# Two tiles of x transposed on the PE, four PSUM banks for the first dense layer, and gate_w on SyncE's queue

## The chip, the core and the metric

The kernel runs on one core of a Trainium2 chip. The metric is the device time of one execution in microseconds. Before the change it is 751.95 us, the median of three runs (751.55 to 753.9).

## What is computed

`x` is [2048, 512] in bf16; the reference is condensed here. The result is a mix of two branches, weighted per row by a gate:

```python
g = _sigmoid((x * gate_w).sum(-1, keepdims=True))
a = _A_ref(x, A_mem0, A_Wq, A_Wk, A_Wv, A_Wo, A_seg_len)   # 64 segments of 32 rows, one after the other
b = _B_ref(x, B_w1, B_b1, B_w2, B_b2)                      # layernorm, 512 -> 1376, gelu, 1376 -> 512
return g * a + (1 - g) * b

# inside _A_ref, for each segment s: 8 memory rows ahead of 32 rows of x
h = jnp.concatenate([mem, xs], axis=1)
q, k, v = h @ Wq, h @ Wk, h @ Wv                           # 32 heads of 128
p = _softmax(where(mask, q @ k.T * scale, -1e9))
o = (p @ v) @ Wo
mem = o[:, :M, :]                                          # feeds the next segment
outs.append(o[:, M:, :])

# inside _B_ref
y = _layernorm(x, axis=-1)
h = _gelu(jnp.einsum('bsd,df->bsf', y, w1) + b1)
return jnp.einsum('bsf,fd->bsd', h, w2) + b2
```

## The kernel before

The program has two stages. The **dense stage** computes branch b. The **recurrent stage** runs over the 64 segments in order; it starts with the projections of tile 0 and takes most of the time. Each engine works its own instruction list in the order in which the code is written; an instruction that must wait holds up all that stands behind it on its engine. Transfers are issued from the lists of SyncE (SP), ScalarE (ACT) and GpSimd (POOL), and their data pass through the same 16 DMA engines.

The dense stage takes x in 16 tiles `T` of 128 rows, two tiles to a block, so 8 blocks of 11 units `fc` (128 of the 1376 hidden columns each). A unit is:

- `a_mm(blk, fc)`, L477: four matmuls of 128x256 into a PSUM bank `hp` (L482), then the gelu on ACT (L483), which frees the bank. Blocks 0 to 6 take turns between the banks `SbF` and `W` (`U[3]` once in block 0); block 7 uses four banks.
- `b_mm(blk, fc)`, L485, issued two units later (`LAG = 2`): for a tile whose second layer is done here, one matmul of 128x512 (L489) that reads the gelu of `fc` and adds into `U[0]` or `U[2]`. The odd tiles and tile 14 (`DEF`) put their gelu into DRAM instead (`spill`, L499, on SP) and take the second layer in the recurrent stage.

At a block's border ACT has two instructions more: the tanh of the gate (`gates`, L469) and `ct_out` (L504), which takes the block's result out of PSUM. DVE makes the next block's normalised rows (`prep`: L437 statistics, a short chain of small operations, `y` at L452). PE transposes `y` into `X1` and `X2` at `fc` 8 and 9 (`prep_tr`, L459), DVE copies that to `yT` (L460), and then DVE forms the gate sums of the block (`junk`, L465, which reads `gw_bc`, the copy of `gate_w` in all partitions).

SP's list in a block: a spill, two loads of recurrent weights of 1024 KB (`loads`, L321), the second spill, two tiles of x for the block after the next (`ld_x`, L317). In block 3 `loads` also issues two DMA transposes (`load_xT`, L102) that bring tiles 0 and 1 of x in transposed form to `xT[0]` and `xT[1]`. The recurrent stage reads them: `first_h` (L507), issued in block 6, has PE transpose the start memory `m0` into the bank `X1`, DVE copy it to `hT` (L511), and POOL copy parts of `xT`.

At the start of the program PE runs 11 matmuls on the identity (`warm`, L526), which compute nothing that is used, then the transposes of `y` of tiles 0 and 1, one of `b1r` (the bias, L535, loaded by POOL), and one more `warm` ahead of the first `a_mm`. POOL also loads `gw_bc` (L344).

Of the kernel before, what the change touches and what calls it, by code (L numbers as in the profile page):

```python
# [10 lines left out]
BF16 = mybir.dt.bfloat16  # L11
# [17 lines left out]
def kernel(ctx, tc, A_x, A_mem0, A_Wq, A_Wk, A_Wv, A_Wo, A_seg_len, B_x, B_w1, B_b1, B_w2, B_b2, gate_w, out):  # L29
    nc = tc.nc  # L30
    P = 128
    _, S, Dm = A_x.shape
# [6 lines left out]
    KC = Dm // P  # L39
# [23 lines left out]
    ident = pers.tile([P, P], BF16)  # L63
# [11 lines left out]
    ew = early.enter_context(tc.tile_pool(name="ew", bufs=2))  # L75
# [24 lines left out]
    def load_xT(T):  # L100
        xT = ew.tile([P, KC, P], BF16, tag="xT", bufs=3, name="xT")
        nc.sync.dma_start_transpose(out=xT[:], in_=x2[T * P:(T + 1) * P, :])  # L102
        xTs[T] = xT
# [7 lines left out]
    U = [lps.tile([P, 512], FP32, name=f"U{i}") for i in range(4)]  # L111
    X1 = lps.tile([P, 512], FP32)
    X2 = lps.tile([P, 512], FP32)
    SbF = lps.tile([P, 512], FP32)
    W = lps.tile([P, 512], FP32)
# [48 lines left out]
    xTs, GLs = {}, {}  # L164
# [136 lines left out]
    with tc.tile_pool(name="mlpw", bufs=1) as mlpw, \  # L301
# [4 lines left out]
        NBLK = NT // TB  # L306
# [4 lines left out]
        gw_bc = mlpw.tile([P, Dm], BF16)  # L311
        hTm = [mout.tile([P, TB, FC, P], BF16, name=f"hTm{i}") for i in range(2)]
        xts = {}
# [6 lines left out]
        def ld_w(W_, A, n):  # L320
            nc.sync.dma_start(W_[:, n, :], A[n * P:(n + 1) * P].rearrange("p h e -> p (h e)"))  # L321

        def ld_o(i):
            nc.sync.dma_start(Wo_sb[:, i:i + 8, :], A_Wo[i:i + 8].rearrange("h e d -> e h d"))
# [7 lines left out]
        NWARM = 11  # L332
        H1, H2, F1 = 3, 6, 7 * P

        def ld_w2(eng, a, b):
            eng.dma_start(w2_sb[:, a:b, :], B_w2[a * P:b * P, :].rearrange("(fc p) d -> p fc d", p=P))
# [4 lines left out]
        ld_x(3)  # L341
        ld_w2(nc.sync, H1, H2)
        nc.sync.dma_start(w1_sb[:, :, F1:F], w1v[:, :, F1:F])
        nc.gpsimd.dma_start(gw_bc[:], gate_w.partition_broadcast(P))  # L344
        ld_w2(nc.sync, H2, H2 + 2)
        ld_w2(nc.sync, H2 + 2, FC - 1)
        nc.sync.dma_start(w2_sb[:FR, FC - 1, :], B_w2[(FC - 1) * P:F, :])
        nc.sync.dma_start(w2_sb[FR:FR + 1, FC - 1, :], B_b2.rearrange("(o d) -> o d", o=1))
        ld_x(4)
# [7 lines left out]

        def loads(blk):
            if blk == 3:
                for T in range(2):  # L360
                    load_xT(T)
                nc.sync.dma_start(m0[:], A_mem0[0])

            for kc in range(2 * blk, min(2 * blk + 2, 3 * KC)):
                ld_w(*((Wv_sb, A_Wv), (Wq_sb, A_Wq), (Wk_sb, A_Wk))[kc // KC], kc % KC)
            if blk == 6:
                for i in range(0, H, 8):
                    ld_o(i)
# [48 lines left out]
        def rsqrt(y, v, n):  # L417
            i1 = msmall.tile([P, n], I32, tag="i1", name="i1")
            nc.vector.tensor_scalar(out=i1[:], in0=v.bitcast(I32), scalar1=1, scalar2=None, op0=ALU.logical_shift_right)
            nc.vector.tensor_scalar(out=y.bitcast(I32), in0=i1[:], scalar1=-1, scalar2=RSQRT_SEED, op0=ALU.mult, op1=ALU.add)  # L420
            for c, a in ((-1.0, RSQRT_A), (-RSQRT_B * RSQRT_B, 5.0)):
                t = msmall.tile([P, n], FP32, tag="nt", name="nt")
                nc.vector.tensor_tensor(out=t[:], in0=y, in1=y, op=ALU.mult)
                nc.vector.scalar_tensor_tensor(out=t[:], in0=t[:], scalar=c, in1=v, op0=ALU.mult, op1=ALU.mult)
                if a == 5.0:
                    nc.vector.scalar_tensor_tensor(out=t[:], in0=t[:], scalar=10.0 / 3.0, in1=t[:], op0=ALU.add, op1=ALU.mult)
                nc.vector.scalar_tensor_tensor(out=y, in0=t[:], scalar=a, in1=y, op0=ALU.add, op1=ALU.mult)
# [3 lines left out]
        def prep(blk):  # L431
            mv = msmall.tile([P, TB, nc.vector.BN_AGGR_DIM], FP32, tag="mv", name="mv")
            ve = msmall.tile([P, TB], FP32, tag="ve", name="ve")
            rs = msmall.tile([P, TB], FP32, tag="rs", name="rs")
            for tt in range(TB):
                st = msmall.tile([P, nc.vector.BN_STATS_DIM], FP32, tag="st", name="st")
                nc.vector.bn_stats(out=st[:], in_=xts[blk * TB + tt][:])  # L437
                nc.vector.bn_aggr(out=mv[:, tt, :], in_=st[:])
                if blk == 0:
                    nc.vector.tensor_scalar(out=ve[:, tt:tt + 1], in0=mv[:, tt, 1:2], scalar1=LN_EPS, scalar2=None, op0=ALU.add)  # L440
                    nc.scalar.activation(out=rs[:, tt:tt + 1], in_=ve[:, tt:tt + 1], func=ACTF.Sqrt)
            if blk == 0:
                nc.scalar.activation(out=dummy[:], in_=ident[:, 0:1], func=ACTF.Gelu_apprx_tanh)
            else:
                nc.vector.tensor_scalar(out=ve[:], in0=mv[:, :, 1], scalar1=LN_EPS, scalar2=1.0 / (RSQRT_K * RSQRT_K), op0=ALU.add, op1=ALU.mult)
                rsqrt(rs[:], ve[:], TB)
            for tt in range(TB):
                T = blk * TB + tt
                if blk == 0:
                    nc.vector.reciprocal(out=rs[:, tt:tt + 1], in_=rs[:, tt:tt + 1])  # L450
                ys[T] = mwork.tile([P, Dm], BF16, tag="y", name="y")
                nc.vector.tensor_scalar(out=ys[T][:], in0=xts[T][:], scalar1=mv[:, tt, 0:1], scalar2=rs[:, tt:tt + 1], op0=ALU.subtract, op1=ALU.mult)  # L452
            yTs[blk] = mwork.tile([P, KC, TB * P], BF16, tag="yT", name="yT")
# [23 lines left out]
        def a_mm(blk, fc):  # L477
            rows = min(P, F - fc * P)
            n = blk * FC + fc
            hp = (SbF, W, U[3], SbF)[n] if n < 4 else (W, SbF, U[2], U[3])[n % 4] if blk == NBLK - 1 else (W, SbF)[n % 2]  # L480
            for kc in range(KC):
                nc.tensor.matmul(hp[:rows, 0:TB * P], lhsT=w1_sb[:, kc, fc * P:fc * P + rows], rhs=yTs[blk][:, kc, :], start=(kc == 0), stop=(kc == KC - 1))  # L482
            nc.scalar.activation(out=hTm[blk % 2][:rows, :, fc, :], in_=hp[:rows, 0:TB * P].rearrange("p (t c) -> p t c", t=TB), func=ACTF.Gelu_apprx_tanh, bias=b1_sb[:rows, fc:fc + 1], scale=1.0)  # L483
# [40 lines left out]
        def warm(n):  # L524
            for _ in range(n):
                nc.tensor.matmul(U[3][:].rearrange("p (a b) -> p a b", a=4), lhsT=ident[:], rhs=ident[:].unsqueeze(1).to_broadcast([P, 4, P]), start=True, stop=True, skip_group_check=True)  # L526

        warm(NWARM)
        prep(0)
        for tt in range(TB):  # L530
            prep_tr(0, tt)
# [221 lines left out]
    for s in range(nseg):  # L753
        T, si = divmod(s, SPT)
# [188 lines left out]
    with tc.If(n_bad > 0, label="general"):  # L943
        with tc.tile_pool(name="gp", bufs=1) as gp, tc.tile_pool(name="gps", bufs=2, space=PSUM) as gps:
# [29 lines left out]
            with tc.For_i(0, NT) as Ti:  # L974
                nc.sync.dma_start(x_sb[:], x2[bass.ds(Ti * P, P), :])
                xo = gps.tile([P, Dm], FP32, tag="xo", bufs=1, name="xo")
                for si in range(SPT):
                    xp = gps.tile([P, KC, seg], BF16, tag="m", name="xpg")
# [81 lines left out]
```

## Time and profile before

| | us |
|---|---|
| median of 3 runs (lowest, highest) | 751.95 (751.55, 753.9) |
| the profiled execution, whole | 755.67 |
| its span, first to last instruction | 753.8 |
| dense stage within the span, to the first projection of tile 0 (L147 at 69.39) | 69.4 |
| ACT busy, DVE busy, POOL busy over the span | 535.6, 399.5, 274.2 |
| DMA | 77.17 MB, mean 102 GB/s |

The profile times one execution; the 1.9 us between its span and its whole time lie around the span. Of the rows that the prediction quotes, the timeline's have the start, the duration, the engine, the line, the operation and the tiles (buffer numbers left out); `x4` means four instructions merged into one row, and brackets at the end say how long the engine had been idle and what ended that. A matmul's duration holds the time until its result has drained, so a row of PE may end after the next one started: the pace of PE is read from starts. PEld is the weight load of PE. In the windows view each row has a stretch, the busy time of PE, PEld, DVE, ACT and POOL with their counts, then the granted TensorE clock, the DMA engines' mean share, and GB/s.

### The profile page before, as it was taken

To read this page: it belongs to the slowest core of one execution; us is meant where nothing else is said; L and a number is where in the kernel's file an instruction comes from. 1 tells how busy PE (TensorE), PEld (TensorE's weight loads), DVE (VectorE), ACT (ScalarE), POOL (GpSimd) and SP (SyncE) were. 2 spreads that over 40 slices of the span, in tenths; PEclk is the share of its full clock that TensorE was granted. 3 is DMA by queue.
4 is the path that set the end of the run, shared out by engine and by line. 5 is a ranking of instruction groups with operands and counts; after the bars stand their busy time and mean duration, and the time that the engine had idled before them with its cause. 6 is when DMAs were issued, how large, how long until landed. Compare 5 with 4: busy or idle time off the path is not lost.

```text
span 753.8 us, 45384 instructions
## 1 busy us (share of the span) xinstructions
PE 736.0 (98%) x19896; PEld 429.8 (57%) x19896; DVE 399.5 (53%) x1415; ACT 535.6 (71%) x1627; POOL 274.2 (36%) x516
## 2 busy tenths in 40 slices
PE   8999999999999999999999999999999999999996
PEld 5776555555555555555555565555555655555553
DVE  6776555446454554445554545445464545555444
ACT  5777667777776776777777777767777777777663
POOL 4001323444324444334433344333443334433341
PEclk9999999999999999999999999999999999999999
DMA  9999323122321323221322313231323222222321
GB/s 312 343 335 362 104 85 87 55 76 72 93 77 46 91 70 96 69 83 53 92 77 80 86 46 93 68 96 67 70 72 86 79 72 78 57 90 74 95 70 37
DMA packets 69997, 77.17 MB, mean 102 GB/s; under 512 B 34873, under 2 KB 59938, under 8 KB 68258
## 3 DMA queue, kind: packets, MB, share of 16 engines
q1 hardware_dynamic: 68802, 72.65, 31.4%
q8 instruction: 157, 2.57, 1.4%
q0 software_dynamic: 448, 1.05, 0.5%
q10 hardware_dynamic: 544, 0.52, 0.3%
q14 instruction: 46, 0.38, 0.2%
HBM read 60.21 MB, written 7.70 MB: 90 GB/s over the span
## 4 chain that ended last, share of the span: by engine, by line
PE 91%; DVE 3%; DMA 2%; issue 2%; ACT 1%; POOL 0%; DVEq 0%; SPq 0%; ACTq 0%; POOLq 0%
PE U L128 33%; PE X L159 19%; PE X L147 17%; PE X L128 4%; PE U L290 3%; PE W L674 3%; PE U L147 2%; PE SbF L482 1%; PE U L266 1%; DMA xt<-in_A_x_dram 1%; PE W L482 1%; PE U L489 1%; DVE junk L465 1%; PE SbF L266 1%; PE SbF L701 1%
## 5 line engine op out<-in xcount | busy, mean ns | idle before, releaser
L730 POOL TENSOR_TENSOR UT<-XR,Rb 128x384 bf16<-128x384 bf16 x126 | 140.2, 1134 | 310.1 <-DMA Rb<-r_dr 252.6
L133 ACT CAST Tb<-U 128x512 bf16<-128x512 f32 x288 | 168.7, 586 | 78.7 <-PE U L128 72.5
L128 PEld LDWEIGHTS <-hT 128*32 128x32 bf16 x4096 | 108.9, 96 | 95.5 <-DVE hT L748 1.1
L147 PE MATMUL X<-Wv_sb,hT 128*32 128x512 bf16 x2048 | 144.9, 378 | 0.9 <-issue 0.9
L128 PE MATMUL U<-Wq_sb,hT 128*32 128x512 bf16 x2048 | 145.1, 380 | 0.0
L128 PE MATMUL U<-Wk_sb,hT 128*32 128x512 bf16 x2048 | 144.6, 379 | 0.0
L159 PE MATMUL X<-Wo_sb,UT 128*32 128x512 bf16 x2016 | 123.0, 380 | 0.2
L748 DVE CAST hT<-U 128x8 bf16<-128x8 f32 x126 | 21.0, 167 | 172.0 <-PE U L746 131.1
L811 ACT CAST V<-X 128x256 bf16<-128x256 f32 x256 | 88.7, 372 | 16.4 <-PE X L147 3.5
L137 DVE STREAM_TRANSPOSE QT<-Tb 128x256 f32<-128x256 f32 x128 | 57.0, 446 | 71.9 <-ACT Tb L133 71.5
L159 PEld LDWEIGHTS <-UT 128*32 128x32 bf16 x2048 | 56.6, 96 | 57.1 <-issue 17.7
L707 ACT CAST XR<-U 128x256 bf16<-128x256 f32 x252 | 78.6, 438 | 0.0
L737 ACT CAST w<-X 128x128 bf16<-128x128 f32 x189 | 44.8, 310 | 45.8 <-PE X L159 45.1
L137 DVE STREAM_TRANSPOSE KT<-Tb 128x256 f32<-128x256 f32 x128 | 57.0, 445 | 25.3 <-ACT Tb L133 25.3
L730 POOL TENSOR_TENSOR UL<-XR,Rb 128x128 bf16<-128x128 bf16 x126 | 60.2, 500 | 0.0
L147 PEld LDWEIGHTS <-hT 128*32 128x32 bf16 x2048 | 47.0, 94 | 22.3 <-issue 1.8
L842 ACT CAST UT<-U 128x64 bf16<-128x64 f32 x252 | 35.3, 227 | 28.2 <-PE U L295 28.2
L722 POOL TENSOR_TENSOR racc<-racc,R 128x72 f32<-128x72 f32 x63 | 21.2, 337 | 93.6 <-DVE R L720 49.9
L674 PE MATMUL W<-w_sb,hm 128*32 128x256 bf16 x728 | 52.7, 273 | 0.1
L794 ACT ACTIVATE E<-U 128x64 bf16<-128x64 f32 (+1 forms) x128 | 35.0, 273 | 11.3 <-PE U L270 11.1
L482 PEld LDWEIGHTS <-w_sb 128*128 128x128 bf16 (+1 forms) x352 | 33.5, 100 | 13.4 <-issue 2.4
L159 PE MATMUL X<-Wo_sb,UL 128*32 128x512 bf16 x512 | 39.8, 379 | 0.2 <-issue 0.2
(178 smaller groups left out, 1223.0 us busy)
## 6 DMA issues: line engine op xcount, KB each, us to landing
Rb<-r_dr SPq DMA_DIRECT2D x63, 512.0 KB, 3.9
Wv_sb<-in_A_Wv_dram SPq DMA_DIRECT2D x4, 1024.0 KB, 7.2
Wq_sb<-in_A_Wq_dram SPq DMA_DIRECT2D x4, 1024.0 KB, 8.5
Wk_sb<-in_A_Wk_dram SPq DMA_DIRECT2D x4, 1024.0 KB, 9.0
Wo_sb<-in_A_Wo_dram SPq DMA_DIRECT2D x4, 1024.0 KB, 9.7
VP<-VL SPq DMA_DIRECT2D x64, 64.0 KB, 3.2
hm<-h_dr SPq DMA_DIRECT2D x91, 32.0 KB, 2.2
c<-c_dr SPq DMA_DIRECT2D x16, 128.0 KB, 3.5
```

Of the source, the lines that this page charges most:

```text
L128: nc.tensor.matmul(bk[32 * j:32 * j + 32, :], lhsT=G[:, kc, :], rhs=W5[t][:, kc, h0:h1, j, :], start=(kc == 0), stop=(kc == KC - 1), tile_ ...
L133: nc.scalar.copy(out=Tb[:], in_=bk.rearrange("p (a b e) -> p a e b", a=8, b=2))
L137: nc.vector.transpose(out=dst[:, 8 * hf:8 * hf + 8, c0:c0 + 32, :].rearrange("p a r b -> p a (r b)").bitcast(FP32), in_=Tb[:].rearrange("p ...
L147: nc.tensor.matmul(bk[32 * j:32 * j + 32, :], lhsT=G[:, kc, :], rhs=Wv5[:, kc, 4 * vb:4 * vb + 4, j, :], start=(kc == 0), stop=(kc == KC - ...
L159: nc.tensor.matmul(bk[32 * c:32 * c + 32, :], lhsT=U_[:, j, i, :], rhs=Wo_sb[:, 4 * i + j, :], start=(n == 0), stop=(n == NW - 1), tile_po ...
L482: nc.tensor.matmul(hp[:rows, 0:TB * P], lhsT=w1_sb[:, kc, fc * P:fc * P + rows], rhs=yTs[blk][:, kc, :], start=(kc == 0), stop=(kc == KC - 1))
L674: nc.tensor.matmul(W[32 * c:32 * c + 32, cc], lhsT=hm[:, 32 * c:32 * c + 32], rhs=w2_sb[:, fc, cc], start=(fc == 0 and h == 0), stop=(fc = ...
L707: nc.scalar.copy(out=XR[:, j], in_=U[j][:, 0:NG * 40].rearrange("p (i q) -> p i q", q=40)[:, :, 0:32])
L730: nc.gpsimd.tensor_tensor(out=out[:, :, 4 * h:4 * h + 4, o:o + b - a], in0=XR[:, :, 4 * h:4 * h + 4, a:b], in1=Rb[:, h, :, :, a:b], op=ALU ...
L737: nc.scalar.copy(out=w[:, a:b], in_=bk[:, a:b])
L811: nc.scalar.copy(out=V[:, i0:i0 + 2, :].rearrange("p i e -> p (i e)"), in_=(X1, X2)[vb][:, 256 * h:256 * h + 256])
L842: nc.scalar.copy(out=UT[s % 2][:, j, :, 0:M], in_=U[j][:, 0:NG * 40].rearrange("p (i q) -> p i q", q=40)[:, :, 32:40])
```

## The change

Three things are changed.

```diff
-        nc.gpsimd.dma_start(gw_bc[:], gate_w.partition_broadcast(P))
         ld_w2(nc.sync, H2, H2 + 2)
         ld_w2(nc.sync, H2 + 2, FC - 1)
+        nc.sync.dma_start(gw_bc[:], gate_w.partition_broadcast(P))
         nc.sync.dma_start(w2_sb[:FR, FC - 1, :], B_w2[(FC - 1) * P:F, :])
...
         def loads(blk):
             if blk == 3:
-                for T in range(2):
-                    load_xT(T)
                 nc.sync.dma_start(m0[:], A_mem0[0])
...
                     nc.scalar.activation(out=rs[:, tt:tt + 1], in_=ve[:, tt:tt + 1], func=ACTF.Sqrt)
+                    if tt == 0:
+                        xp_out(0)
             if blk == 0:
                 nc.scalar.activation(out=dummy[:], in_=ident[:, 0:1], func=ACTF.Gelu_apprx_tanh)
+                xp_out(1)
...
-            hp = (SbF, W, U[3], SbF)[n] if n < 4 else (W, SbF, U[2], U[3])[n % 4] if blk == NBLK - 1 else (W, SbF)[n % 2]
+            hp = (SbF, W, U[1], U[3])[n % 4]
...
+        def xp(T):
+            tp = U[T][:].bitcast(BF16)[:, 0:Dm].rearrange("p (k t) -> p k t", k=KC)
+            for kc in range(KC):
+                nc.tensor.transpose(tp[:, kc, :], xts[T][:, kc * P:(kc + 1) * P], ident[:])
+
+        def xp_out(T):
+            xTs[T] = ew.tile([P, KC, P], BF16, tag="xT", bufs=3, name="xT")
+            nc.scalar.copy(out=xTs[T][:], in_=U[T][:].bitcast(BF16)[:, 0:Dm].rearrange("p (k t) -> p k t", k=KC))
+
-        warm(NWARM)
+        warm(NWARM - 6)
+        xp(0)
+        warm(2)
+        xp(1)
+        warm(3)
         prep(0)
```

`xp` transposes the raw tiles 0 and 1 on PE, four transposes each, into `U[0]` and `U[1]`; `xp_out` has ACT copy them to `xT`. PE's list at the start becomes 5 `warm`, 4 transposes, 2 `warm`, 4 transposes, 3 `warm`, and then as before the transposes of `y`.

On ACT at the start of the program, before (the tiles: `rs` is the root of the variance, `dummy` a one-column operation that brings a function table in, `hTm` the gelus of block 0; U_118 to U_121 are `U[0]` to `U[3]`):

```order
L522 ACT_TABLE_LOAD
L522 ACTIVATE dummy<-ident 128x1
L441 ACTIVATE rs<-ve 128x1 x2
L443 ACT_TABLE_LOAD
L443 ACTIVATE dummy<-ident 128x1
L483 ACTIVATE hTm_144<-SbF,b_sb 128x2x128
L483 ACTIVATE hTm_144<-W,b_sb 128x2x128
L483 ACTIVATE hTm_144<-U_121,b_sb 128x2x128
L483 ACTIVATE hTm_144<-SbF,b_sb 128x2x128
```

and of the change at the same place:

```order
L523 ACT_TABLE_LOAD
L523 ACTIVATE dummy<-ident 128x1
L439 ACTIVATE rs<-ve 128x1
L536 COPY xT<-U_118 128x512
L439 ACTIVATE rs<-ve 128x1
L443 ACT_TABLE_LOAD
L443 ACTIVATE dummy<-ident 128x1
L536 COPY xT<-U_119 128x512
L484 ACTIVATE hTm_144<-SbF,b_sb 128x2x128
L484 ACTIVATE hTm_144<-W,b_sb 128x2x128
L484 ACTIVATE hTm_144<-U_119,b_sb 128x2x128
L484 ACTIVATE hTm_144<-U_121,b_sb 128x2x128
```

One copy stands between the two roots, the other between the table load and the first gelu; no table load is added, and the gelus read four banks in turn.

On SP at the start, before (`w_sb` stands for both weights: L330, L339 and L343 are w1, L336 and L347 w2):

```order
L330 DMA w_sb<-in_B_w_dram 128x4x384
L339 DMA w_sb<-in_B_w_dram 128x4x512
L317 DMA xt<-in_A_x_dram 128x512 x2
L336 DMA w_sb<-in_B_w_dram 128x3x512
L343 DMA w_sb<-in_B_w_dram 128x4x480
L336 DMA w_sb<-in_B_w_dram 128x2x512 x2
L347 DMA w_sb<-in_B_w_dram 96x512
```

and of the change, from the same w1 load on:

```order
L343 DMA w_sb<-in_B_w_dram 128x4x480
L336 DMA w_sb<-in_B_w_dram 128x2x512 x2
L346 DMA gw_bc<-in_gate_w_dram 128x512
L347 DMA w_sb<-in_B_w_dram 96x512
L348 DMA w_sb<-in_B_b_dram 1x512
```

The load of `gw_bc` now stands behind the last part of w1 and nearly all of w2.

On SP in block 3, before:

```order
L102 DMA_TRANSPOSE xT<-in_A_x_dram 128x4x128 x2
L362 DMA m_168<-in_A_mem_dram 8x512
L321 DMA Wq_sb<-in_A_Wq_dram 128x4096 x2
L499 DMA h_dr_72<-hTm_145 128x640
L317 DMA xt<-in_A_x_dram 128x512 x2
```

and of the change:

```order
L500 DMA h_dr_72<-hTm_145 128x768
L360 DMA m_168<-in_A_mem_dram 8x512
L321 DMA Wq_sb<-in_A_Wq_dram 128x4096 x2
L500 DMA h_dr_72<-hTm_145 128x640
L317 DMA xt<-in_A_x_dram 128x512 x2
```

The two DMA transposes are gone from between the spill of block 3 and the loads of `m0` and Wq.

## The prediction

> **What bounds the kernel now.** First the head of the page and its chain of waits.
>
> ```profile
> span 753.8 us, 45384 instructions
> ...
> PE 736.0 (98%) x19896; PEld 429.8 (57%) x19896; DVE 399.5 (53%) x1415; ACT 535.6 (71%) x1627; POOL 274.2 (36%) x516
> ...
> PE 91%; DVE 3%; DMA 2%; issue 2%; ACT 1%; POOL 0%; DVEq 0%; SPq 0%; ACTq 0%; POOLq 0%
> ```
>
> TensorE sets the end, so the change is worth what it takes out of PE's idle time. All its edits lie in the dense stage, so I read that stage next: the windows view, then the timeline at every place where PE stands still.
>
> ```profile
> 8.00:48.00 40.00, 39.19 (x319) 28.98 (x317) 30.52 (x113) 27.91 (x63) 3.62 (x12) 1.00 0.98 329
> ```
>
> Two things are full here, PE (39.19 of 40 us) and the DMA engines (share 0.98). A gain on PE must not run into late transfers. Where PE stops at a block's border (timeline; the last two rows are from the chain of waits and give PE's pace):
>
> ```profile
> 17.98 0.47 ACT L483 ACTIVATE hTm<-SbF,b_sb 128x256 bf16<-128x256 f32 x1
> 17.98 0.38 PE L489 MATMUL U<-w_sb,hTm 128*128 128x512 bf16 x1
> 18.50 0.60 PE L482 MATMUL SbF<-yT,w_sb 128*128 128x256 bf16 x4
> ...
> 57.77 0.38 PE L489 MATMUL U<-w_sb,hTm 128*128 128x512 bf16 x1
> 58.27 0.60 PE L482 MATMUL W<-yT,w_sb 128*128 128x256 bf16 x4
> ...
> 19.10 0.21 PE U L489
> 19.31 0.44 PE W L482 x4
> ```
>
> A `b_mm` takes PE 0.21 us and an `a_mm` 0.44. The `b_mm` at 17.98 is over for PE at 18.19, yet the next `a_mm` starts at 18.50, just after the gelu of 17.98 has ended (18.45) and freed its bank. That gelu is late because ACT did the tanh and `ct_out` first. PE loses 18.50 - 18.19 = 0.31 us, and in block 6 58.27 - 57.98 = 0.29 us. The same pair stands in each of blocks 1 to 6: six stops of 0.30 us.
>
> **Part 1, four banks: 5 x 0.30 = 1.5 us in blocks 1 to 5.** With four banks the `a_mm` of 18.50 can start at 18.19 and ends at 18.63. Behind it stands the `b_mm` of the unit two back, which reads the gelu that ends at 18.45: 0.18 us to spare, so the wait isn't merely moved. If ACT were later by more than that, the excess would come back. What is late next is DVE's `y` for the transposes at `fc` 8:
>
> ```profile
> 44.81 0.74 DVE L452 TENSOR_SCALAR y<-xt,mv,rs 128x512 bf16<-128x512 bf16 x2
> 45.63 0.39 PE L459 MATMUL X<-ident,y 128*128 128x128 bf16 x4
> ```
>
> The first `y` is done about 45.18 (half of 0.74), PE comes at 45.63 and would come 0.30 earlier, since DVE starts its chain at the block's beginning and PE saves its time after that: 0.15 us are left. I take the whole 0.30 per block; the ends are 0.15 (DVE eats half) and 0.31. Block 7 already uses four banks and gains nothing.
>
> **Part 2, no DMA transposes: 0.57 us in block 6, with the bank's share.**
>
> ```profile
> 36.65 2.65 SPq L102 DMA_TRANSPOSE xT<-in_A_x_dram  x2
> ...
> 37.00:42.00 5.00, 5.00 (x44) 3.82 (x43) 3.69 (x12) 3.58 (x9) 0.00 (x0) 1.00 0.94 175
> 42.00:50.00 8.00, 7.88 (x65) 5.78 (x63) 6.14 (x22) 5.74 (x14) 0.54 (x1) 1.00 1.00 370
> ```
>
> While the two transposes run, the engines are as busy as ever (0.94) but move 175 GB/s; afterwards 370. The lost 5 x 195 = 975 KB are 2.6 us of transfer time, and all later loads queue behind it. It reaches PE in block 6:
>
> ```profile
> 48.82 8.81 DMA xt<-in_A_x_dram
> ...
> 57.66 0.69 DVE L437 BATCH_NORM_STATS2 st<-xt 128x6 f32<-128x512 bf16 x1 [0.57 <-DMA xt<-in_A_x_dram]
> 61.61 0.38 PE L489 MATMUL U<-w_sb,hTm 128*128 128x512 bf16 x1
> 62.05 0.17 DVE L511 COPY hT<-X 128x32 bf16<-128x32 bf16 x1
> 62.27 0.38 PE L459 MATMUL X<-ident,y 128*128 128x128 bf16 x4 [0.28 <-DVE hT L511]
> ```
>
> Tiles 14 and 15 need 8.81 us to land; DVE's statistics wait 0.57 us for them; the copy of `m0` out of `X1` (62.05) stands behind `y` on DVE; and PE, free at 61.61 + 0.21 = 61.82, may write `X1` only at 62.27. With the tiles in time, DVE's chain moves up 0.57 and the transpose to 61.70. PE, without its bank stop, is there at 61.53 and waits 0.17. So block 6 gains 62.27 - 61.70 = 0.57 for both edits. The tiles must land 0.57 + 1.5 us earlier: SP issues them behind the spills, which follow PE, so their issue moves up by the 1.5, and 2.6 us less queue covers the rest. Ends: 0 (tiles late by the same) and 0.74 (no wait left).
>
> The 2.65 us that SP saves in issuing are worth nothing by themselves: what stands behind is the loads just counted.
>
> **Part 3, the start: +0.33 us.** PE, DVE and ACT in the first 9 us, and a cast of the new copy's size from the page:
>
> ```profile
> 1.47 4.87 PE L526 MATMUL U<-ident 128*128 128x512 bf16 x11 [1.47 <-POOL ident masks.py:199]
> 3.59 0.69 DVE L437 BATCH_NORM_STATS2 st<-xt 128x6 f32<-128x512 bf16 x1 [3.59 <-DMA xt<-in_A_x_dram]
> 5.73 0.20 ACT L441 ACTIVATE rs<-ve 128x1 f32<-128x1 f32 x1 [0.80 <-DVE ve L440]
> 6.27 0.42 PE L459 MATMUL X<-ident,y 128*128 128x128 bf16 x4
> 6.72 0.94 DVE L460 COPY yT<-X 128x512 bf16<-128x512 bf16 x2
> 7.57 0.16 PE L535 MATMUL U<-ident,b1r 11*128 11x11 bf16 x1 [0.36 <-DMA b1r<-in_B_b_dram]
> 7.89 0.60 PE L482 MATMUL SbF<-yT,w_sb 128*128 128x256 bf16 x4
> 8.53 0.47 ACT L483 ACTIVATE hTm<-SbF,b_sb 128x256 bf16<-128x256 f32 x1 [1.08 <-PE SbF L482]
> ...
> L133 ACT CAST Tb<-U 128x512 bf16<-128x512 f32 x288 | 168.7, 586 | 78.7 <-PE U L128 72.5
> ```
>
> The copies: 0.59 us each. The first goes into the 0.80 us in which ACT waits ahead of the second root, the other into the 1.08 us ahead of the first gelu; it is over by about 8.05, before `a_mm` 2 needs `U[1]` at 7.89 + 2 x 0.44 = 8.77. Hidden; without that cover 0.59 each.
>
> PE: a `warm` takes 4.87 / 11 = 0.44 us, half the pace of a 128x512 matmul later (0.21), so the clock is still low; the transposes of `y` at 6.27 (0.42 for four with the drain) are past that. Five `warm` end at 3.67, when tile 0 has landed (3.59). Eight transposes at the low clock are a quarter of a `warm` each, 0.88 in all; ten `warm` are 4.4. PE is free between 6.4 (the last `warm` at full clock) and 6.9 with late weight loads, against 6.27: 0.1 to 0.6 late. `yT` is done at 6.72 + 0.94 = 7.66, but the first `a_mm` waits to 7.89, since the bias's transpose waits for its load: 0.2 us of cover. I take 0.1 us of delay, with ends 0 and 0.4.
>
> `gw_bc` (timeline, then DMA issues):
>
> ```profile
> 3.53 0.58 POOL L344 DMA_DIRECT2D gw_bc<-in_gate_w_dram  x1
> 6.80 1.55 SPq L347 DMA_DIRECT2D w_sb<-in_B_w_dram  x1
> 11.81 0.38 PE L489 MATMUL U<-w_sb,hTm 128*128 128x512 bf16 x1
> 12.47 0.33 PEld L482 LDWEIGHTS <-w_sb 128*128 128x128 bf16 x4 [0.67 <-DMA w_sb<-in_B_w_dram]
> 15.43 0.68 DVE L465 SCALAR_TENSOR_TENSOR junk<-xt,gw_bc 128x512 bf16<-128x512 bf16 x1
> ...
> gw_bc<-in_gate_w_dram POOLq DMA_DIRECT2D x1, 128.0 KB, 6.6
> w_sb<-in_B_w_dram SPq DMA_DIRECT2D x1, 96.0 KB, 7.4
> ```
>
> PE, free at 11.81 + 0.21 = 12.02, stands until 12.47 for the last part of w1. The 128 KB of `gw_bc` landed at 3.53 + 6.6 = 10.1, ahead of it; at 370 GB/s they are 0.35 us. With them behind, w1 lands 0.35 earlier, and PE goes on at 12.13 (12.02 + 0.1 of delay, or 12.12 by the load): gain 0.33. Ends: 0 (w1 no earlier, or PE 0.4 late) and 0.45. In its new place `gw_bc` should land like the w2 load beside it, 6.80 + 7.4 = 14.2, and is read at 15.43: 1.2 us to spare.
>
> A rule of the Trainium skill speaks against the new start: its page TensorE: Matmul & The Clock Gate, Part 4: PE-mode transpose, has it that a PE transpose doesn't count as PE-busy for the clock gate in the way a matmul does. No row here shows transposes during the ramp, so the trace can't say. By the rule the sum would go the way of the second rival, without it this part stays at 0.33.
>
> **Sum:** 1.5 + 0.57 + 0.33 = 2.4 us, to be seen as a span of 751.4 in place of 753.8. The profiled execution (755.67 with what lies around the span) is 3.7 us above the median; the same 2.4 off the median 751.95 gives **749.55 us**.
>
> **Rivals.**
>
> 1. *The DMA engines become the bound.* A block moves 2 x 1024 + 2 x 128 + 192 + 160 + 128 KB (weights, x, two spills, one result), 2.85 MB, or 7.7 us at 370 GB/s; a block takes 7.96 us now (26.46 - 18.50 in the chain, below) and would take 7.66. For it: the share of 0.98. Against: 2.6 us of queue are taken away. If the tiles land late again in blocks 3 to 6, 0.9 of the banks' share and the 0.57 go: 2.4 - 1.5 = 0.9, so 751.05.
>
> ```profile
> 18.50 0.60 PE SbF L482 x4
> 26.46 0.60 PE W L482 x4
> ```
>
> 2. *The clock stays low: slower.* The ramp took from 1.47 to 6.27 at most, 4.8 us of unbroken matmuls. If transposes break it, it starts anew behind the last of them: PE's start comes 1 us later (warm-ups and transposes at half pace to the end), and 4.8 us of dense work at half pace lose 2.4. Less the 0.45 of waiting for w1 that this hides, the start costs 2.95 in place of a gain of 0.33: 2.07 - 2.95 = -0.9, so 752.85; if the next pause of PE (the weight load of 12.47) breaks the ramp once more, 2.4 more, 755.25. Each us of dense work at the low clock costs 0.5, so it decides from a clock that rises later than about 12 us. Against: 5 + 2 + 3 `warm` still fill most of the stretch. (The rule of the Trainium skill named above would lead here.)
>
> 3. *Four banks do nothing,* since `b_mm` waits for the same gelu. For: ACT's order is unchanged. Against: the 0.18 us. It would take back the 1.5: 751.05.
>
> **How the numbers follow.** Forecast 0.68, rivals 0.14, 0.08 and 0.10. PE also has waits in the recurrent stage that the profile puts to nothing:
>
> ```profile
> PE U L290 <- issue: 3.2, 5, 1.0
> ```
>
> Single ones are up to 1.0 us, and they may fall otherwise in a program with other instructions ahead. All gains at their upper ends are 5 x 0.31 + 0.74 + 0.45 = 2.74 (749.2), all at their lower ones 0.75 (751.2). The forecast's own range is 748.3 (the upper ends and one such wait less) to 750.6 (not all the lower ends at once); with the first and third rival the range is 748.3 to 751.3. A measurement of this kernel tells about 0.3%, 2.26 us, from no change, so faster by more means below 749.69, close to the forecast. I give 0.7 of its 0.68 to that side, because the upper ends of w1's wait and of block 6 are nearer than their lower ones and more transfer time comes free than I count, and 0.02 of the rivals: faster 0.50. Slower by more (above 754.2) is the second rival with its second pause, 0.06. Same 0.44.
>
> **What would show it.** Right: the `a_mm` at `fc` 4 of blocks 1 to 6 starts 0.21 us after the `b_mm` ahead; no stretch near 38 us below 300 GB/s; no DVE wait for `xt` ahead of block 7; the wait for w1 under 0.15 us; the first projection of tile 0 near 67.0 in place of 69.39. Wrong: `b_mm` waiting for gelus (rival 3), `st` waiting for `xt` (rival 1), matmuls at 0.43 us pace behind 7.9 us (rival 2), `junk` waiting for `gw_bc`, or a gain at 67 us that is lost again before the end.

## The result and the profile after

The changed kernel takes 748.92 us, the median of 21 runs (746.27 to 752.41); the kernel before, measured beside it, 751.24 (748.8 to 755.97). The ratio is 0.9966, with a 95% interval of 0.9952 to 0.9981: 2.6 us less, between 1.4 and 3.6. The forecast was 749.55 us. Its total was met, but two of its three terms came out otherwise than argued, and one of its rivals was nearer than it was held to be.

The heads of the page of the changed kernel (span and instructions; busy time of each engine):

```profile
span 748.0 us, 45397 instructions
...
PE 733.3 (98%) x19903; PEld 434.8 (58%) x19903; DVE 399.4 (53%) x1415; ACT 536.8 (72%) x1629; POOL 273.6 (37%) x515
```

The dense stage can be read block by block. The table has, for block 0, the start of its first dense matmul. For every later block it has the start of the `a_mm` right behind the last `b_mm` of the block before, which is the one at `fc` 2, since `b_mm` runs two units later. Below that stands the first projection of tile 0 (L147). All are from the timeline of PE in the two profiled executions:

| us | before | after | length before | length after |
|---|---|---|---|---|
| block 0 | 7.89 | 8.15 | 9.01 | 8.53 |
| block 1 | 16.90 | 16.68 | 7.96 | 7.65 |
| block 5 | 48.74 | 47.28 | 7.94 | 7.65 |
| block 6 | 56.68 | 54.93 | 8.69 | 8.68 |
| block 7 | 65.37 | 63.61 | 4.02 | 4.03 |
| tile 0's first projection | 69.39 | 67.64 | | |

Blocks 1 to 5 together: 48.74 + 7.94 - 16.90 = 39.78 us before, 54.93 - 16.68 = 38.25 after. So the gain of 1.75 us at the end of the stage is 0.48 (block 0) + 1.53 (blocks 1 to 5) + 0.01 (block 6) - 0.01 (block 7) - 0.26 (a later start). The first and the last of these belong together: a later start leaves less to wait for behind it, and the two make 16.90 - 16.68 = 0.22 us.

**A block's border**, from the timeline of PE:

```profile
17.77 0.38 PE L490 MATMUL U<-w_sb,hTm 128*128 128x512 bf16 x1
17.98 0.60 PE L483 MATMUL U<-yT,w_sb 128*128 128x256 bf16 x4
```

The `a_mm` at 17.98 now follows the `b_mm` of 17.77 after 0.21 us, that matmul's own time. Before, the same pair stood at 17.98 and 18.50.

**The stretch of the former DMA transposes**, from the windows view (stretch, length, busy us of PE, PEld, DVE, ACT and POOL, clock, DMA share, GB/s):

```profile
8.00:48.00 40.00, 40.00 (x330) 30.51 (x331) 31.70 (x117) 29.08 (x67) 3.01 (x8) 1.00 0.99 362
36.00:41.00 5.00, 5.00 (x45) 3.82 (x43) 3.97 (x12) 3.66 (x9) 0.00 (x0) 1.00 0.98 369
```

369 GB/s where there were 175 (from 37 to 42 us, the place of the transposes before), and PE without a stop from 8 to 48 us. But the DMA share is 0.99, no less than before: what was freed is filled.

**The start and block 6**, from the timeline of PE, DVE and POOL:

```profile
7.83 0.16 PE L549 MATMUL U<-ident,b1r 11*128 11x11 bf16 x1 [0.76 <-DMA b1r<-in_B_b_dram]
8.15 0.60 PE L483 MATMUL SbF<-yT,w_sb 128*128 128x256 bf16 x4
...
56.41 0.54 POOL L506 DMA_DIRECT2D c_dr<-ct  x1 [7.11 <-ACT ct L505]
57.00 0.75 POOL L107 COPY GL<-xT 128x128 bf16<-128x128 bf16 x2
57.55 0.27 POOL L245 COPY hT<-xT 128x96 bf16<-128x96 bf16 x1
...
57.01 0.84 DVE L446 TENSOR_SCALAR ve<-mv 128x2 f32<-128x2 f32 x1
59.66 0.74 DVE L453 TENSOR_SCALAR y<-xt,mv,rs 128x512 bf16<-128x512 bf16 x2
60.31 0.17 DVE L512 COPY hT<-X 128x32 bf16<-128x32 bf16 x1
...
60.53 0.38 PE L460 MATMUL X<-ident,y 128*128 128x128 bf16 x4 [0.58 <-DVE hT L512]
```

The 0.57 us for which `st` waited for tiles 14 and 15 are gone (no such bracket stands ahead of block 7 any more), and yet PE stops ahead of the same transpose, now for 0.58 us. DVE's operation on two numbers per row, `ve`, took 0.84 us in place of 0.17. It started at 57.01, 0.01 us behind the first of three copies on POOL, and ended at 57.85; the last of the copies ended at 57.82. So the copies are the first suspect.

The spans differ by 753.84 - 748.02 = 5.8 us, of which the dense stage explains 1.75. The other 4.07 lie in the recurrent stage, whose instructions the change leaves alone, and have to be held against what that stage does from one execution to the next.

### The profile page after: what moved, and what is told of

Read it like the earlier page. It is cut to its first block, busy times and chain, and to the rows that moved or that the text cites. A ratio compares the mean times of both kernels' runs of the same rounds, so it can differ in the third digit from the quotient of the medians.

```text
span 748.0 us, 45397 instructions
## 1 busy us (share of the span) xinstructions
PE 733.3 (98%) x19903; PEld 434.8 (58%) x19903; DVE 399.4 (53%) x1415; ACT 536.8 (72%) x1629; POOL 273.6 (37%) x515
## 4 chain that ended last, share of the span: by engine, by line
PE 95%; DVE 2%; DMA 1%; issue 1%; ACT 1%; POOL 0%; DVEq 0%; POOLq 0%
PE U L128 34%; PE X L159 19%; PE X L147 17%; PE X L128 4%; PE U L290 3%; PE W L688 3%; PE U L483 2%; PE U L490 2%; PE U L147 2%; PE U L266 1%; PE SbF L483 1%; PE W L483 1%; PE SbF L266 1%; DMA b1r<-in_B_b_dram 1%; PE SbF L715 1%
## 5 line engine op out<-in xcount | busy, mean ns | idle before, releaser
L128 PEld LDWEIGHTS <-hT 128*32 128x32 bf16 x4096 | 110.9, 96 | 93.5 <-DVE hT L762 1.2
L147 PE MATMUL X<-Wv_sb,hT 128*32 128x512 bf16 x2048 | 144.8, 378 | 0.0
L147 PEld LDWEIGHTS <-hT 128*32 128x32 bf16 x2048 | 47.5, 94 | 20.9 <-issue 0.7
L128 PE MATMUL U<-Wk_sb,GL 128*32 128x512 bf16 x496 | 39.9, 377 | 0.0
```

The costliest lines, as they stand in the source:

```text
L128: nc.tensor.matmul(bk[32 * j:32 * j + 32, :], lhsT=G[:, kc, :], rhs=W5[t][:, kc, h0:h1, j, :], start=(kc == 0), stop=(kc == KC - 1), tile_ ...
L147: nc.tensor.matmul(bk[32 * j:32 * j + 32, :], lhsT=G[:, kc, :], rhs=Wv5[:, kc, 4 * vb:4 * vb + 4, j, :], start=(kc == 0), stop=(kc == KC - ...
```

## The experiments

Each stage time below is from one profiled execution; ratios are against the kernel before on the same chip. "First projection" is L147's start, 69.39 before and 67.64 after.

### One part alone: four banks

The kernel before, with this line:

```
-            hp = (SbF, W, U[3], SbF)[n] if n < 4 else (W, SbF, U[2], U[3])[n % 4] if blk == NBLK - 1 else (W, SbF)[n % 2]
+            hp = (SbF, W, U[1], U[3])[n % 4]
```

> The kernel before with the four-bank rotation alone; the DMA transposes and the load of gate_w stay as they were. The prediction's Part 1 says that blocks 1 to 5 take 7.65 us each in place of 7.95, and nothing else moves: first projection of tile 0 at 69.39 - 1.5 = 67.9, 1.5 us less in all. Its third rival says that the blocks stay at 7.95 (69.4). Its first rival (the DMA engines become the bound) says that PE's gain meets the late tiles: tiles 14 and 15 landed at 57.63 in the kernel before, behind a queue that moved only 175 GB/s from 37 to 42 us, and if they land at the same time here, the statistics of block 7 wait 0.57 + 1.5 = 2.1 us and block 6 gives most of the 1.5 back (first projection at 69.0 to 69.4). I expect something between the last and the first: the wait for the tiles grows to about 1.2 us, the first projection stands near 68.5.

Measured: blocks 1 to 4 take 7.65 us each, block 5 takes 9.59, and the first projection stands at 69.79, no earlier than before. DVE's and PE's timeline:

```profile
49.80 0.69 DVE L437 BATCH_NORM_STATS2 st<-xt 128x6 f32<-128x512 bf16 x1 [1.87 <-DMA xt<-in_A_x_dram]
...
53.99 0.40 PE L459 MATMUL X<-ident,y 128*128 128x128 bf16 x4 [1.97 <-DVE y L452]
```

The windows view of the five microseconds of the transposes, in this kernel:

```profile
37.00:42.00 5.00, 4.92 (x43) 3.84 (x42) 3.95 (x12) 3.76 (x10) 0.54 (x1) 1.00 1.24 163
```

163 GB/s. PE came earlier, the tiles 12 and 13 did not, and one wait of 1.97 us took the gain of four borders. It was worse than I expected (1.2 us). The ratio was 0.9972 (0.9952 to 0.9992), 12 runs: faster in all, about 2.1 us, though the dense stage of the profiled execution gained nothing. Where the other executions gained is not on record.

### One part alone: transposes on PE

The kernel before with the last two pieces of the diff (`xp`, `xp_out`, the warm-up in parts) and without `load_xT` in block 3.

> The kernel before with the transposes of the first two tiles on PE alone; banks and gate_w as before. The stretch near 38 us should move more than 300 GB/s and the wait of 0.57 us for tiles 14 and 15 should be gone. By the prediction's Part 2, block 6 then gains up to 0.57 us less the bank's share of 0.29, some 0.3 us, and the first projection stands at about 69.1. By the reading of the changed kernel's trace (GpSimd's two copies of GL, right behind the issue of the result's DMA, hold DVE's small operation on the variance back: 0.84 us in place of 0.17), DVE is again held to the end of these copies, which start when PE's block border allows and not when the tiles land; block 6 gains 0.1 at most: first projection at 69.3 to 69.4, and the variance's row takes 0.5 us or more.

Measured: no wait for `xt` in the whole stage, the first projection at 69.01. DVE and POOL at the end of block 6's statistics, and then the window of the former transposes:

```profile
58.53 0.17 DVE L446 TENSOR_SCALAR ve<-mv 128x2 f32<-128x2 f32 x1
58.73 0.67 DVE L417 TENSOR_SCALAR i<-ve 128x2 int32<-128x2 int32 x1
...
58.54 0.77 POOL L107 COPY GL<-xT 128x128 bf16<-128x128 bf16 x2
59.11 0.27 POOL L245 COPY hT<-xT 128x96 bf16<-128x96 bf16 x1
```

```profile
37.00:42.00 5.00, 4.95 (x42) 3.66 (x42) 3.69 (x12) 3.65 (x9) 0.00 (x0) 1.00 0.93 327
```

Here `ve` began 0.01 us ahead of the copies and took its usual 0.17; the operation behind it was held instead, 0.67 us, until 59.40, and the copies ended at 59.38. So the reading stands, with one correction: it isn't the variance that is held, but whichever small operation comes second to the copies. Block 6 gained 0.19 us (8.50), between the two figures expected, and block 0 0.27 (8.74), which I hadn't expected of it: PE started 0.07 later, and the last part of w1 let it go on at 12.28 in place of 12.47. Ratio 0.9973 (0.9953 to 0.9993), 12 runs.

### One part alone: gate_w on SyncE

```
-        nc.gpsimd.dma_start(gw_bc[:], gate_w.partition_broadcast(P))
         ld_w2(nc.sync, H2, H2 + 2)
         ld_w2(nc.sync, H2 + 2, FC - 1)
+        nc.sync.dma_start(gw_bc[:], gate_w.partition_broadcast(P))
```

> The kernel before with the load of gate_w on SyncE alone. By the prediction's Part 3 the wait for the last part of w1 falls from 0.45 to about 0.1 us of PE's time and the first projection stands 0.35 earlier, at 69.05. Also open: the load of the bias landed at 7.43 in the kernel before and at 7.70 in the changed one, which cost PE's start 0.26 us. If the moved load is the reason, it lands near 7.70 here as well; if the transposes are, or chance, near 7.43.

Measured: PE no longer waits for w1, and block 0 takes 8.54 us in place of 9.01. The bias landed at 7.29 us, so the moved load alone doesn't delay it. The first projection nevertheless stands at 69.83, since tiles 12 and 13 came 1.29 us late. The 0.47 us of block 0 were gone again 40 us later, by a wait that the kernel before shows too in its second execution (below).

### Does a transpose raise PE's clock?

In the changed kernel, the warm-up:

```
-                nc.tensor.matmul(U[3][:].rearrange("p (a b) -> p a b", a=4), lhsT=ident[:], rhs=ident[:].unsqueeze(1).to_broadcast([P, 4, P]), start=True, stop=True, skip_group_check=True)
+                for k in range(4):
+                    nc.tensor.transpose(U[3][:].bitcast(BF16)[:, k * P:(k + 1) * P], ident[:], ident[:])
```

> The changed kernel with each warm-up matmul replaced by four transposes of the identity, 128x128 each, which take PE as long. If PE's clock rises with transposes as with matmuls, all stays: y's transposes near 6.25 with 0.39 us for four, the first dense matmuls at 8.15 with 0.44 us per group, first projection near 67.7. If transposes don't raise the clock, the first dense matmuls run at half pace for as long as the ramp lasted before (up to 4.8 us): 0.87 us per group behind 8.15, and the first projection about 2 us later, near 69.7. The Trainium skill, page TensorE: Matmul & The Clock Gate, Part 4: PE-mode transpose, states the second: a transpose on PE doesn't count as PE-busy for the clock gate as a matmul does.

Measured, PE's timeline:

```profile
1.48 2.31 PE L528 MATMUL U<-ident 128*128 128x128 bf16 x20 [1.48 <-POOL ident masks.py:199]
...
6.44 0.40 PE L460 MATMUL X<-ident,y 128*128 128x128 bf16 x4
...
7.89 0.60 PE L483 MATMUL SbF<-yT,w_sb 128*128 128x256 bf16 x4
8.32 0.60 PE L483 MATMUL W<-yT,w_sb 128*128 128x256 bf16 x4
```

Twenty transposes from 1.48 to 3.70 are 0.11 us each; the dense matmuls from 7.89 to 8.32 take 0.43 for a group of four, full pace. Nothing but transposes ran before, and the pace doubled all the same. (The granted clock reads 1.00 in the windows of these first microseconds, here as in the kernel before, so the slow start can only be read from the pace.) The rule of the Trainium skill that the prediction's second rival leaned on (TensorE: Matmul & The Clock Gate, Part 4: PE-mode transpose) doesn't hold for these transposes; the profile lists them as MATMUL and doesn't show their mode. The first projection stands at 67.19, 0.45 earlier than in the changed kernel, because the bias happened to land at 7.35 and block 6 took 8.51.

### GpSimd's copies out of the way

In the changed kernel, out of `first_h` (block 6) to the place behind `prep(0)`:

```
-            for T in range(2):
-                left_x(T)
-            prep_h(0)
...
         prep(0)
+        for T in range(2):
+            left_x(T)
+        prep_h(0)
```

> The changed kernel with GpSimd's three copies out of the transposed tiles (two of GL, one of hT) issued in block 0, where they run beside DVE's statistics, in place of block 6. If these copies hold DVE's small operations back, the variance's row in block 6 is back at 0.17 us, from it to y are 2.0 us as in the other blocks (2.65 in the changed kernel), the stop of 0.58 us ahead of the transpose of the second last tile is 0.1 or less, block 6 lasts about 8.1 us in place of 8.68, and the first projection stands 0.55 earlier (67.1 with the start of the changed kernel). If DVE's chain is late for another reason, block 6 stays at 8.68. Were every operation of DVE held back, the statistics of block 0 would show it (0.69 and 0.66 us now).

Measured, POOL and DVE in block 0, then DVE in block 6:

```profile
9.03 0.75 POOL L107 COPY GL<-xT 128x128 bf16<-128x128 bf16 x2
9.58 0.28 POOL L245 COPY hT<-xT 128x96 bf16<-128x96 bf16 x1
...
9.02 0.66 DVE L435 BATCH_NORM_STATS2 st<-xt 128x6 f32<-128x512 bf16 x1
9.72 0.18 DVE L436 BATCH_NORM_AGGREGATE mv<-st 128x2 f32<-128x6 f32 x1
...
57.10 0.17 DVE L446 TENSOR_SCALAR ve<-mv 128x2 f32<-128x2 f32 x1
59.09 0.73 DVE L453 TENSOR_SCALAR y<-xt,mv,rs 128x512 bf16<-128x512 bf16 x2
```

Beside the statistics the copies cost nothing (0.66 us as ever). In block 6, `ve` is back at 0.17, from it to `y` are 1.99 us in place of 2.65, PE doesn't stop, and block 6 takes 8.00 in place of 8.68. The first projection is at 67.06, although this execution started 0.12 later. The collision is the cause of the lost gain.

### The same copies one block earlier

```
+                if blk == NBLK - 3 and fc == 4:
+                    for T in range(2):
+                        left_x(T)
+                    prep_h(0)
                 if blk == NBLK - 2 and fc == 4:
                     first_h()
```

> The changed kernel with the same three copies one block earlier: they then start behind the issue of block 4's result, near 49.3 us, just as DVE comes to block 5's variance. If the copies hold DVE back, the lengthening moves with them: from the variance to y about 2.6 us in block 5, PE stops about 0.5 us ahead of the transposes there (block 5 about 8.15 in place of 7.65), and block 6 lasts 8.1 in place of 8.68; the first projection is where it was. If something in block 6 itself is the reason, block 5 stays at 7.65 and block 6 at 8.68.

Measured, POOL and DVE in block 5:

```profile
50.41 0.77 POOL L107 COPY GL<-xT 128x128 bf16<-128x128 bf16 x2
50.98 0.27 POOL L245 COPY hT<-xT 128x96 bf16<-128x96 bf16 x1
...
50.40 0.17 DVE L446 TENSOR_SCALAR ve<-mv 128x2 f32<-128x2 f32 x1
50.60 0.68 DVE L417 TENSOR_SCALAR i<-ve 128x2 int32<-128x2 int32 x1
```

The stall moved with the copies: 0.68 us, until 51.28, and the copies ended at 51.25. Block 5 takes 8.11, block 6 takes 8.00. Unexpected: tiles 10 and 11 came 0.79 us late and block 4 took 8.49, so the first projection stands at 68.47.

### The transposes by DMA again, all else as changed

```
             if blk == 3:
+                for T in range(2):
+                    load_xT(T)
                 nc.sync.dma_start(m0[:], A_mem0[0])
...
-        warm(NWARM - 6)
-        xp(0)
-        warm(2)
-        xp(1)
-        warm(3)
+        warm(NWARM)
```

> The changed kernel with the transposes by DMA again: banks and gate_w as in the change. By the prediction's Part 2 it loses 0.57 us in block 6 and nothing else: first projection near 68.2. By what the kernel with the banks alone showed (a wait of 1.87 us for tiles 12 and 13 in block 5), the stretch near 38 us moves little, the tiles are late by 1.5 to 2 us, and the first projection stands near 69.5: then the PE transposes are what lets the banks' gain stand.

Measured: first projection at 70.96, 3.3 us later than in the changed kernel. DVE and PE:

```profile
49.83 0.69 DVE L437 BATCH_NORM_STATS2 st<-xt 128x6 f32<-128x512 bf16 x1 [2.11 <-DMA xt<-in_A_x_dram]
...
54.02 0.40 PE L459 MATMUL X<-ident,y 128*128 128x128 bf16 x4 [1.98 <-DVE y L452]
...
56.93 1.06 PE L482 MATMUL U<-yT,w_sb 128*128 128x256 bf16 x4
```

Tiles 12 and 13 are 2.11 us late, PE stops for 1.98, and the matmuls behind that ran at half pace until 57.8 (56.93 to 57.78 for a group that takes 0.44 elsewhere). Block 5 took 11.45 us in place of 7.65: 2.0 of waiting and about 1.7 of slow clock, an estimate from the granted clock of 0.78 from 54 to 55 us and 0.50 or 0.51 from 55 to 58. Block 6 took 8.17 in place of 8.68. This is one execution; how late the tiles are changes from one to the next (below).

### Towards a version that beats both

The kernel with the early copies and, besides, `a_mm`'s first group ahead of the bias's transpose:

```
+            if n == 0:
+                b1p = U[2][:].bitcast(BF16)[:, 0:FC]
+                nc.tensor.transpose(b1p, b1r[:], ident[:FC, :FC])
+                nc.vector.tensor_copy(out=b1_sb[:], in_=b1p)
             nc.scalar.activation(out=hTm[blk % 2][:rows, :, fc, :], in_=hp[:rows, 0:TB * P].rearrange("p (t c) -> p t c", t=TB), func=ACTF.Gelu_apprx_tanh, bias=b1_sb[:rows, fc:fc + 1], scale=1.0)
...
-        b1p = U[2][:].bitcast(BF16)[:, 0:FC]
-        nc.tensor.transpose(b1p, b1r[:], ident[:FC, :FC])
-        nc.vector.tensor_copy(out=b1_sb[:], in_=b1p)
-        warm(1)
```

> The changed kernel with the early copies of GpSimd and, besides, the first group of dense matmuls ahead of the bias's transpose, so that PE no longer waits for the bias's load (0.36 us before, 0.76 in the changed kernel). The first dense matmul should start when yT is done, near 7.6 in place of 8.15, with no wait for gelus behind it: block 0's first second-layer matmul 0.4 to 0.5 us earlier, block 6 at 8.1: first projection near 66.7 in place of 67.6, 0.9 to 1.0 us less in all than the changed kernel, 3.4 less than before (ratio 0.995 to 0.996 to the kernel before). If the gelus wait for the bias instead, the start gains nothing and 0.55 us are left.

Measured: ratio 0.9939 (0.9916 to 0.9961), 6 runs. The first dense matmul started at 7.75, 0.40 us earlier than in the changed kernel, but block 0's first `b_mm` at 9.27, only 0.19 earlier (9.46), not the 0.4 to 0.5 expected: the bias's transpose stands behind the first group now, and the second group starts 0.64 us behind the first in place of 0.44. Besides, tiles were late again, here ahead of block 7; PE's and DVE's timeline:

```profile
7.75 0.60 PE L483 MATMUL SbF<-yT,w_sb 128*128 128x256 bf16 x4 [0.52 <-DVE yT L461]
...
56.20 0.69 DVE L435 BATCH_NORM_STATS2 st<-xt 128x6 f32<-128x512 bf16 x1 [0.53 <-DMA xt<-in_A_x_dram]
```

Block 0 takes 8.74 us (8.53 in the changed kernel), blocks 4 and 6 take 8.05 and 8.62, and the first projection is at 67.90, not the 66.7 expected. The windows view of the stage:

```profile
8.00:67.00 59.00, 58.24 (x483) 44.02 (x481) 46.68 (x178) 42.73 (x100) 5.48 (x14) 1.00 1.00 355
```

The DMA engines are full over the whole stage (share 1.00), so that a PE that comes earlier meets transfers that don't. That this is why the gain was lost is argued from the late tiles, not shown by itself.

The next kernel shifts the recurrent weights by one part, in `loads`:

```
-            for kc in range(2 * blk, min(2 * blk + 2, 3 * KC)):
+            for kc in range(max(2 * blk - 1, 0), min(2 * blk + 1, 3 * KC)):
```

> The kernel of e9_both with the loads of Wv, Wq and Wk one part later: block 0 issues one part in place of two, block 6 the last one, so that every pair of x tiles has 1 MB (2.8 us at 370 GB/s) less ahead of it in the queue. If the waits for tiles in e9_both (0.53 us ahead of block 7) and in the changed kernel's second execution (0.38) come from the weights ahead of them, no wait for xt is left, blocks 1 to 5 take 7.65 each, block 6 8.0, the first matmul stands near 7.7 and the first projection at 66.3 to 66.7; Wk's last part should land near 65, ahead of its use behind 68. In all 1.2 us less than the changed kernel, 3.7 less than before: ratio near 0.995. If the tiles are late for another reason, a wait of 0.3 to 0.6 stays. If Wk comes late, the stop is at its first use, behind 68 us.

Measured: ratio 0.997 (0.9953 to 0.9987), 12 runs; first projection at 67.19. The wait for tiles 14 and 15 only fell to 0.28 us, and the queue asked for the rest later, in PE's timeline of the first segment:

```profile
80.98 0.21 PE L295 MATMUL U<-E,VP 32*128 32x64 bf16 x4 [1.99 <-DMA VP<-VL]
```

The weights' parts themselves were in time, but `Wo` and the spills behind it were pushed back on SP (the last issue of `Wo` ended at 70.1 us, 67.0 in the kernel without the shift), and a small transfer of `VP` that the first segment needs, issued at 76.0 in place of 72.2, landed too late. Behind that stop the granted clock was low, which cost about 1.7 us more (last section). A miss, and a price that the expectation hadn't looked for: it named Wk as the load at risk.

Beside it ran the changed kernel.

> The changed kernel beside the last one on the same chip, for the difference of the two: 1.2 us more by the dense stage, which is less than a ratio of 0.002 and may stay within the intervals. Dense stage as in its first two executions: first projection at 67.6 to 67.8.

Measured: ratio 0.9934 (0.9912 to 0.9956), 6 runs; first projection at 67.47. Neither of the two versions is faster than the change by what these runs can tell; the one with the weights later has the higher median, 751.70 us beside 748.99.

### The two kernels again

> The changed kernel once more, for what changes by itself from one execution to the next. What the mechanism sets should come again: blocks 1 to 5 at 7.65, the variance's row in block 6 lengthened, no wait for the last tiles. What is chance should move: the landing of the bias (7.29 to 7.70 so far), and the length of the recurrent stage behind 72.8 us (675.2 here, 679.3 in the kernel before, 676.3 to 677.9 in the others).

> The kernel before once more. What the mechanism sets should come again: blocks 1 to 5 at 7.96, a stretch near 38 us that moves under 260 GB/s, a wait for tiles 14 and 15 of some tenths. The length of the recurrent stage (679.3 us in the first execution, 675 to 678 in all the others) should come out below 679 if that one was drawn long by chance, and near 679 if the change itself shortens that stage.

Measured, DVE's first statistics of a block that waited, in the changed kernel and then in the kernel before:

```profile
55.87 0.69 DVE L435 BATCH_NORM_STATS2 st<-xt 128x6 f32<-128x512 bf16 x1 [0.38 <-DMA xt<-in_A_x_dram]
```

```profile
50.18 0.69 DVE L437 BATCH_NORM_STATS2 st<-xt 128x6 f32<-128x512 bf16 x1 [1.11 <-DMA xt<-in_A_x_dram]
58.40 0.70 DVE L437 BATCH_NORM_STATS2 st<-xt 128x6 f32<-128x512 bf16 x1 [0.51 <-DMA xt<-in_A_x_dram]
```

The wait for tiles is drawn anew in each execution: 0.17 and 0.57 us in the first of the kernel before, 1.11 and 0.51 in the second; none, 0.38 and 0.17 in three of the changed one. So each of the two expectations missed in one point: the changed kernel's second execution did wait for the last tiles, and block 5 of the kernel before took 8.82 us in place of 7.94. The first projection stands at 69.39 and 70.19 before (mean 69.79), at 67.64, 67.77 and 67.47 after (mean 67.63). So the dense stage gains 2.2 us on average, more than the 1.75 of the first pair.

The recurrent stage (from the first step's start to the end of the span) took 679.3 and 678.3 us in the kernel before, 675.2, 676.4 and 674.8 in the changed one. Kernels with the DMA transposes gave 676.3 (banks), 677.2 (`gate_w`) and 675.5 (all but the transposes); kernels with those on PE gave 677.9 (alone), 676.3 (warm-up), 676.4, 672.6 and 675.9 (early copies, a block early, both edits), and 679.0 with the weights later, of which 2.0 are its new wait and about 1.7 the slow clock behind it. The second execution of the kernel before is not below 678, but the groups overlap and no single part of the change brings the difference. Whether the change shortens that stage is not settled.

## Why the prediction was right in its total, and where it was not

**What bounds.** PE sets the end, as said. "Two things are full here" was the more important half of that sentence: with PE's stops taken out, the DMA queue decides whether a block takes 7.65 us.

**Part 1 (1.5 us)** came out as worked out, in the changed kernel: 0.31 us per block, 1.53 in five blocks, and neither ACT nor DVE took any of it. The third rival fell: no `b_mm` waits for a gelu.

**Part 2 (0.57 us, in block 6)** has the right cause and the wrong place. The transposes by DMA do thin the queue out, and without them the wait for tiles 14 and 15 is gone or smaller. The step that failed is "With the tiles in time, DVE's chain moves up 0.57 and the transpose to 61.70". DVE's chain moved up into GpSimd's three copies. In the kernel before, the late tiles had kept the two nearly apart: by the time DVE came to `ve`, the copies were nearly over.

```profile
59.29 0.27 POOL L245 COPY hT<-xT 128x96 bf16<-128x96 bf16 x1
59.40 0.19 DVE L445 TENSOR_SCALAR ve<-mv 128x2 f32<-128x2 f32 x1
```

`ve` ended at 59.59, 0.03 us behind the last copy. So two waits ended together there, and the prediction listed only the one for the tiles; with the tiles in time the copies held DVE to the same point of the block (they ended 2.88 us into block 6 before, 2.89 after). In the three executions of the changed kernel `ve` took 0.84, 0.38 and 0.59 us, and block 6 took 8.68 or 8.69 each time, as in both executions of the kernel before: what sets it is the end of the copies, not the landing of the tiles. The end 0 of the range for this term is what came, in block 6: 0.01 us. Moved copies gave 0.68 (8.68 to 8.00), which shows the price.

What the term left out is larger than what it held. It priced the DMA transposes by the one wait seen in one execution. Tiles 12 and 13 stopped PE in block 5 in four of the five executions with the DMA transposes (0.69, 1.09, 1.97 and 1.98 us), and in none of the nine without them, of which two had a stop for tiles in block 4 (0.67 and 0.23). Put back into the changed kernel, the transposes cost 3.3 us in the one execution taken, about 1.7 of it by the slow clock. The sum added the terms as if each stood by itself; in these executions Part 1's gain lasted to the end of the stage only together with Part 2. The totals don't show that: the banks alone were as much faster, by their 12 runs, as the transposes alone.

**Part 3 (+0.33 us)** came out at 0.22 (block 1 at 16.68 in place of 16.90). The move of `gate_w` does what was argued: alone, it let PE through without a wait, and block 0 was over at 16.29. No `junk` waited for it, and ACT's two copies were hidden. The step that was mis-sized is the delay of the start: 0.1 us was taken, and 0.26 came in the first execution (0.28 and 0.10 in the two others). A later start also shortens the wait for w1 by itself: with the banks alone PE started at 8.23, and block 0 took 8.67 with `gate_w` where it had been, yet ended at the same 16.90. So the 0.48 us that block 0 lost are not all due to the moved load. The late start was not the transposes: the ramp was over in time, and `yT` was done at 7.53. The bias landed at 7.70. Over the kernels of this study it landed anywhere from 7.29 to 7.92, with and without transposes and the moved load. "0.2 us of cover" was read off a landing that is chance.

**The rivals.** The first (DMA engines as the bound) was given 0.14, and was put down with "2.6 us of queue are taken away". The runs show it in a milder form: late tiles in two of three executions of the changed kernel and in the version that starts PE earlier. Its full form, the banks' gain lost, is what happens with the banks alone. The second (a clock that stays low) fell twice, in the changed kernel and with a warm-up of nothing but transposes.

**The total.** 2.4 us were forecast; the dense stage gained 1.75 in the profiled pair and 2.2 on average, the measured ratio says 2.6 (1.4 to 3.6). That the total was met so closely is partly luck: in the profiled pair two of the terms fell short by 0.67 us together, and 4.07 us lie in a stage for which the sum has no term. The 21 runs of the changed kernel alone spread over 6 us, more than the whole effect, so that the total can't tell how good the terms were; only the stage's own rows can. (The range's lower end, 749.2 less one wait of 1.0, is 748.2 and not 748.3.)

## What to carry to other kernels

Where two resources are both full, the terms of a sum don't stand alone: ask of each edit whether the other resource lets its gain through, and look at more than one execution before a transfer's landing carries a term. When a wait goes, read which operations of other engines the waiting one now runs beside; here a late load had kept DVE's small operations clear of GpSimd's copies. Work on GpSimd that must run beside DVE goes best beside the operations that it doesn't hold up, here the statistics.

## What the runs showed of the hardware

**GpSimd's copies hold DVE's small operations to their very end.** In all eleven executions in which the copies ran beside these operations, the one that was held ended 0.02 or 0.03 us behind the last of the three copies: 57.85 against 57.82, 59.40 against 59.38, 51.28 against 51.25, 61.58 against 61.55 in the changed kernel with the DMA transposes, and so on. One that came first by 0.01 us took its usual 0.17 (at 58.53 and 50.40). The Trainium skill (SBUF — State Buffer, Who interferes with whom) has this: DVE's two-port modes and GpSimd share a port pair, whoever issues first holds it, and the other is blocked fully. The trace agrees on the order and the block, here for operations of two numbers per row, which are held over all three copies and not only one; the mode in which they ran is not in the trace. The statistics beside the same copies weren't held (0.66 us).

**The same pause of PE may or may not cost its clock.** A pause of 1.97 us left the pace as it was in the kernel with the banks alone; a pause of 1.98 in the one with the DMA transposes put back halved it, and so did the pause of 1.99 in the kernel with the weights later. Windows of these two show the granted clock (the column ahead of the DMA share):

```profile
55.00:56.00 1.00, 1.00 (x7) 0.77 (x6) 0.11 (x1) 0.47 (x1) 0.00 (x0) 0.50 1.03 373
56.00:57.00 1.00, 1.00 (x6) 0.64 (x5) 0.97 (x4) 0.20 (x1) 0.00 (x0) 0.50 1.16 458
```

```profile
82.00:83.00 1.00, 1.00 (x16) 0.36 (x12) 0.00 (x0) 1.00 (x4) 0.00 (x0) 0.50 0.58 131
83.00:84.00 1.00, 1.00 (x16) 0.45 (x12) 0.00 (x0) 0.05 (x1) 0.00 (x0) 0.50 0.14 20
```

Both were low for about 3.4 us, an estimate from such windows (54 to 58 and 81 to 85 us). What decides whether a pause costs the clock stays open.

**Two DMA transposes of 128 KB each** kept the queue at 140 to 176 GB/s for five microseconds in every execution that had them (with a share of 0.84 to 1.24), against 327 in the kernel before with those on PE and 369 in the changed one.
